# Three blocks in one kernel: two token lists for the experts, list numbers read by GpSimd, and a first phase in a new order

## The chip, the cores and the metric

The kernel runs on one core of a Trainium2 chip. The metric is the device time of one launch, in microseconds (us); the time before is the median of three runs. Engines: TensorE (PE, and PEld for its weight loads), VectorE (DVE), ScalarE (ACT), GpSimd (POOL), and SyncE (SP), which only issues transfers. SPq and POOLq are the queues of SP and GpSimd.

## What is computed

Three independent results, all in float32 at the interface:

```python
# 1. gated linear attention, B=4 H=8 S=768 D=48; a = complex gate, limited to |a| <= 0.999
for t in range(S):
    S_re, S_im = a[t] * (S_re + i S_im) + k[t] outer v[t]
    y[t] = q[t] @ S_re
# 2. a dense block on x of N=3072 rows, DM=384, DFF=2048
y = softplus(x @ w_in) @ w_out
# 3. eight experts, top 1, on N=3072 rows, F2=1024
e_idx = argmax(x @ w_gate + modality_bias[modality_id])
out[mask_e] = gate_w[mask_e] * (relu(x[mask_e] @ w1[e]) @ w2[e])
```

Here the three are chained: the attention's y is the x of the dense block, and its y is the x of the experts.

## The kernel before

All three blocks are matmuls whose operands are split into a high and a low part (`xh`, `xl`, `w`, `gh`, `gl`), three products each. The work has two phases.

**Phase 1** (to about 743 us) runs attention, the dense block, the router and three early pairs of expert tiles interleaved. Each is written as generators (`Attn`, `Moe1`, `Early`) that announce their next operation (`Op`: engine, estimated duration, what it needs, ring places it takes, due unit). `Streams.run` (L148) asks all of them for the time at which they could start, takes the engine that can start first, and among that engine's candidates the one with the smallest `due - LEAD`. A candidate may be chosen although it starts up to `PATIENCE` nanoseconds later than the first. `LEAD` has three numbers a stream, for the first unit, the middle and the last; a stream that has no entry has zeros. The result is a fixed order of instructions for each engine. The clock that `run` advances (`end`, L122) knows an engine's duration, a bus for transfers and at most eight transfers in flight; a transfer counts as landed 900 ns after the bus has moved it.

Tokens go in 24 tiles of 128 (`n`); two tiles make a unit `m` of 256 tokens (12 units) and a group `g` of the attention (12 groups). Of a group:

- `decays` and `products` (L255, L331) make gates and gated q and k on VectorE and ScalarE. The last product, L380, releases 24 loads by SP's queue (`stack`, L390: 12 for each tile, 6 of `ks`, 6 of `qs`), which lay k and q out by head.
- `scores` (L399): TensorE's `pa` (L414) needs the `ks` and `qs` of the tile; VectorE masks the result (`at`, L422).
- `outputs` (L439): `py` on TensorE; ScalarE and VectorE copy it to `y` (L465, L468); two moves on SP's queue (L480, y<-y) turn it; `sink` (L576) splits it into `xh` (L585, ScalarE) and `xl` (L587, VectorE).
- The dense block: `hs` (L613), `softplus` (L626 to L637), `gh` (L644), `gl` (L652), `ys` (L669 to L671).
- The router (`router_unit`, L690): rank of each token within its expert (`pr`, L725 to L729), then its place `di` (L758), and two scatters by GpSimd, one for each tile of the unit, which write the token numbers (`tok`) into a DRAM list `lst` at these places (L762). Both write the same tensor, so that the second waits until the first has landed. `x2d`, L740, stores the tokens' rows.

`Early` takes three pairs of tiles of 256 tokens when ten of the twelve units are routed: a table of offsets, the list entries (`fids`, L1166 to L1168, SP), gathers (`fx`, GpSimd), transposes (`fxt`), weights (`fes`, `few0h/l`, `few1h/l`), first products (`feh`, L1248), relu (`frh` L1259, `frl` L1261), second products (`fey`, L1279), results (`fo`, L1289) and their scatter to `out` (L1292). In names such as `frl13` or `few0l21` the first figure of the last two is the pair and the second the quarter of its hidden columns.

**Between the phases** VectorE makes the table of the remaining pairs (`table`, L796, some 50 small operations up to L872) when the last unit is ranked. `begin` (L1034) loads the first weights (`est`), splits them (`w0h`, `w0l`, `w1h`, `w1l`; L931, L936), reads the lists of the first three pairs (`load_ids`, L893, SP) and gathers their rows (`gather`, L905), and transposes the first pair (`ext`, L954; `exh`, `exl`). **Phase 2** (`Moe2.run`, L1070) is ordered by hand: `eh` (L976), relu, `ey` (L1024), results, scatter to `out` (L1031). A list is read on SP's queue at an offset that SP loads from the table:

```python
o = nc.sync.value_load(self.c["tab"][0:1, 1, s:s + 1], min_val=0, max_val=E * RS)
nc.sync.dma_start(ids[:, :n], self.lst[bass.ds(o, n * P)].rearrange("(p k) o -> p (k o)", k=n))
```

Of the kernel before, what the change touches and what calls it, by code (L numbers as in the profile page):

```python
# [24 lines left out]
P = 128  # L25
# [30 lines left out]
LEAD = dict(load_a=(40.235, 77.705, -53.959), load_qk=(5.175, 62.509, -31.682), decays=(16.662, -1.332, -76.619), products=(1.104, -28.277, -61.848), scores=(-31.933, 17.078, -33.279), outputs=(-39.509, 5.144, 14.553), load_w=(-26.207, 60.684, -77.629), split_w=(46.815, 84.855, 60.651), gate_w=(31.817, -31.456, 89.703), hs=(2.837, 86.252, 46.309), logs=(61.552, 28.125, -11.984), softplus=(53.029, 53.679, -34.061), highs=(-86.34, 1.631, -25.826), lows=(26.821, 19.731, -34.925), ys=(-12.292, -83.704, -79.285), evac=(-55.587, 17.06, 15.15), router=(-2.963, -42.318, 24.777), prepare=(1.018, 90.264, 20.598))  # L56
PATIENCE = (36, 0, 148)
# [4 lines left out]
class Op:  # L62
# [5 lines left out]
    def __init__(self, eng, ns, after=None, take=(), key=None, free=(), lat=None, due=None,  # L68
                 rows=1.0, moves=()):
        self.moves = moves  # L70
# [18 lines left out]
def dma(xfer, k=1, ns=470, **kw):  # L89

    return Op("S", k * ns, moves=[xfer] * k, **kw)

# [8 lines left out]
class Streams:  # L101
# [82 lines left out]
class Attn:  # L184
# [8 lines left out]
    def __init__(self, tc, ctx, a_in, qk_in, v_in, consts, psum):  # L193
# [10 lines left out]
        self.first = self.wp.tile([P, H * 64], F32, tag="v", name="first")  # L204
# [291 lines left out]
class Moe1:  # L496
# [193 lines left out]
    def router_unit(self, m):  # L690
# [80 lines left out]
class Moe2:  # L771
# [133 lines left out]
    def gather(self, s):  # L905
        nc = self.nc
        ids = self.rows[s][0]
# [126 lines left out]
    def begin(self, dynamic=True):  # L1034
# [17 lines left out]
        def tokens():  # L1052
            for s in self.order[:3]:
                yield dma(50, 1, 1500, after=["table", ("lst", NM - 1)], key=("fi", s), due=NM)
                self.load_ids(s)
            for s in self.order[:3]:
                yield Op("G", 1300 * 2, after=[("fi", s), ("x2d", NM - 1)], key=("fx", s), lat=3000)
# [64 lines left out]
class Early:  # L1122
# [11 lines left out]
    def table(self):  # L1134
# [27 lines left out]
    def tokens(self):  # L1162
        nc = self.nc
        for j in range(NE):
            yield dma(50, 1, 1500, after=["early table", ("lst", EU - 1)], key=("ei", j), due=NM + j)
            o = nc.sync.value_load(self.c["early"][0:1, 1, j:j + 1], min_val=0, max_val=E * RS)  # L1166
            self.ids[j] = self.p.tile([P, 2], I32, tag="ids", name=f"fids{j}", bufs=NE)
            nc.sync.dma_start(self.ids[j], self.lst[bass.ds(o, 2 * P)].rearrange("(p k) o -> p (k o)", k=2))  # L1168

    def gathers(self):  # L1170
        for j in range(NE):
            place = Place("ex")
            yield Op("G", 1300 * 2, after=[("ei", j), ("x2d", EU - 1)], take=[place], key=("fg", j), lat=3000, due=NM + j)
# [108 lines left out]
    def evac(self):  # L1282
# [12 lines left out]
    def streams(self):  # L1295
        return (self.table(), self.tokens(), self.gathers(), self.xts(), self.loads(), self.splits(), self.mm1s(), self.relus(),
                self.mm2s(), self.evac())
# [102 lines left out]
def build(ctx, tc, i, out):  # L1400
# [6 lines left out]
    lst = dr.tile([E * RS + 2 * P, 1], I32, name="lst")  # L1407
# [16 lines left out]
    def prepare(room):  # L1424

        n = (E * RS + 2 * P) // P
        pad, mi, rest = room[:, :n].bitcast(I32), room[:, 256:256 + 2 * NT].bitcast(I32), room[:, 320:]
        zero, bb, mf, fl = [rest[:, k * 32:(k + 1) * 32] for k in range(4)]
# [10 lines left out]
        yield dma(120, 4, key="given")  # L1439
# [3 lines left out]
        nc.sync.dma_start(lst.rearrange("(p k) o -> p (k o)", p=P), pad)  # L1443
# [18 lines left out]
    with ExitStack() as s2:  # L1462
        with ExitStack() as s1, ExitStack() as sr, ExitStack() as se, ExitStack() as sa, ExitStack() as sw, tc.manual_schedule():
# [26 lines left out]
            def late():  # L1490
# [4 lines left out]
                for g in ex.begin():  # L1495
# [6 lines left out]
                        prepare(attn.first), early(), late())  # L1502
# [45 lines left out]
def slow(ctx, tc, i, c, dr, x2d, lst, out):  # L1548
# [6 lines left out]
    with ExitStack() as s:  # L1555
# [6 lines left out]
        nc.sync.dma_start(lst.rearrange("(p k) o -> p (k o)", p=P), pad)  # L1562
# [30 lines left out]
def host_inputs(q, k, v, a_re, a_im, moe_w_in, moe_w_out, moe2_modality_id, moe2_w_gate, moe2_modality_bias,  # L1593
# [22 lines left out]
        "tok": tok.T.astype(i32),  # L1616
# [23 lines left out]
```

## Time and profile before

| | us |
|---|---|
| median of three runs | 999.04 |
| the three runs | 994.08, 999.04, 1004.93 |
| the profiled execution | 1004.99 |
| its span | 1003.2 |
| its mean granted clock | 0.973 of full speed |

The profile is of one execution. Busy times are of instructions of an engine; a number in square brackets behind a row is the engine's idle time just before it, and what released it. "x8" says how many instructions a row stands for. In the table of stretches PEclk is the granted TensorE clock, in parts of full speed. Durations of transfers in SPq rows are the time that the queue was occupied with issuing them. The program's names stand without their numbers; the figures of a tile behind a name are left out in the trace.

### The profile page before, as it was taken

Reading aid. Unit: us, or ns where it says so; the run is one execution under the profiler, and the core shown is the slowest. Engines: PE = TensorE matmul, PEld = TensorE weight load, DVE = VectorE, ACT = ScalarE, POOL = GpSimd, SP = SyncE. Lnnn points to the kernel's source line nnn. Section 1 sums busy time; section 2 is a strip of 40 time slices with the busy share of each in tenths; the row PEclk is TensorE's granted clock in tenths of the full one; section 3 lists DMA queues with packets and bytes.
Section 4 is the critical chain, followed back from the end, with each engine's and each line's share of the span. In section 5 each row is a group of like instructions: output and inputs, shape, how many; then the busy total and the mean of one; then the engine's idle time right before and its main releaser. Section 6 shows DMA issues by size and latency. Waiting matters only on the chain. (4 is left out here: it accounts for less than half of the span.)

```text
span 1003.2 us, 17451 instructions
## 1 busy us (share of the span) xinstructions
PE 867.9 (87%) x6377; PEld 827.2 (82%) x6377; DVE 765.9 (76%) x1682; ACT 588.5 (59%) x1041; POOL 91.8 (9%) x94
## 2 busy tenths in 40 slices
PE   1544688999899989999988999999987989999993
PEld 1334688989898889999887899989976989999983
DVE  6999798999799989999877798354467356566582
ACT  4554376575757575766755746465554356555682
POOL 0000000000000000000000000021016022221120
PEclk9999899999999999999989999999998989999997
DMA  9602304141414231332322331251285563542640
GB/s 338 278 1 57 126 25 128 43 126 46 123 40 129 51 118 43 126 101 68 95 74 61 77 91 47 77 151 43 64 289 190 189 245 124 170 150 97 221 163 17
DMA packets 71379, 115.37 MB, mean 115 GB/s; under 512 B 12438, under 2 KB 54989, under 8 KB 68722
## 3 DMA queue, kind: packets, MB, share of 16 engines
q1 hardware_dynamic: 66930, 103.80, 32.2%
q0 software_dynamic: 4352, 10.36, 3.2%
q8 instruction: 52, 0.85, 0.4%
q14 instruction: 45, 0.37, 0.2%
HBM read 93.85 MB, written 10.44 MB: 104 GB/s over the span
## 5 line engine op out<-in xcount | busy, mean ns | idle before, releaser
L613 PE MATMUL h<-xh,w 128*128 128x256 f32 x1152 | 223.2, 287 | 15.7 <-DVE t L637 10.8
L613 PEld LDWEIGHTS h<-xh,w 128*128 128x128 f32 x1152 | 185.0, 192 | 21.2 <-DVE t L637 13.3
L613 PE MATMUL h<-xl,w 128*128 128x256 f32 x576 | 164.1, 285 | 2.9 <-DVE xl L587 2.8
L669 PE MATMUL y<-w,gh 128*128 128x392 f32 x384 | 137.1, 357 | 0.7 <-ACT gh L644 0.7
L671 PE MATMUL y<-w,gl 128*128 128x392 f32 x384 | 131.4, 342 | 1.7 <-DVE gl L652 1.7
L670 PE MATMUL y<-w,gh 128*128 128x392 f32 x384 | 131.4, 342 | 0.0
L613 PEld LDWEIGHTS h<-xl,w 128*128 128x128 f32 x576 | 110.4, 192 | 4.1 <-DVE xl L587 4.1
L626 ACT ACTIVATE t<-h 128x512 f32<-128x512 f32 x96 | 57.1, 595 | 70.9 <-PE h L613 44.7
L762 POOL DMA_INDIRECT lst<-c_tok,di x24 | 25.9, 1078 | 678.0 <-DVE di L758 623.8
L936 DVE TENSOR_TENSOR w1l<-est,w1h 128x768 fp32r<-128x768 f32 x52 | 47.9, 953 | 51.4 <-ACT w1h L931 42.2
L652 DVE TENSOR_TENSOR gl<-t,gh 128x512 fp32r<-128x512 f32 x96 | 65.9, 687 | 20.1 <-ACT gh L644 19.8
L637 DVE SCALAR_TENSOR_TENSOR t<-h,t 128x512 f32<-128x512 f32 x96 | 65.9, 686 | 17.2 <-ACT t L630 15.6
L644 ACT CAST gh<-t 128x512 fp32r<-128x512 f32 x96 | 59.2, 618 | 33.3 <-PE y L670 25.1
L669 PEld LDWEIGHTS y<-w,gh 128*128 128x128 f32 x384 | 72.6, 189 | 3.9 <-issue 2.7
L671 PEld LDWEIGHTS y<-w,gl 128*128 128x128 f32 x384 | 72.3, 188 | 3.0 <-DVE gl L652 2.9
L670 PEld LDWEIGHTS y<-w,gh 128*128 128x128 f32 x384 | 72.6, 189 | 0.0
L976 PE MATMUL eh<-exh,w0h 128*128 128x256 f32 x216 | 61.6, 285 | 4.5 <-DVE erl L980 4.5
L414 PE MATMUL pa<-qs,ks 96*128 96x128 f32 x384 | 53.5, 295 | 13.3 <-DMA qs<-qk 9.5
L414 PEld LDWEIGHTS pa<-qs,ks 96*128 96x128 f32 x384 | 49.1, 206 | 17.3 <-issue 9.8
L628 ACT ACTIVATE t<-t 128x512 f32<-128x512 f32 x96 | 60.7, 633 | 2.0
L630 ACT ACTIVATE t<-t 128x512 f32<-128x512 f32 x96 | 60.8, 633 | 1.8
L976 PE MATMUL eh<-exl,w0h 128*128 128x256 f32 x216 | 61.7, 286 | 0.0
(377 smaller groups left out, 2175.5 us busy)
## 6 DMA issues: line engine op xcount, KB each, us to landing
est<-in_w SPq DMA_DIRECT2D x26, 1536.0 KB
raw<-in_w SPq DMA_DIRECT2D x16, 768.0 KB
a<-in_a SPq DMA_DIRECT2D x12, 768.0 KB
qk<-in_qk SPq DMA_DIRECT2D x12, 768.0 KB
ks<-a SPq DMA_DIRECT2D x144, 64.0 KB
qs<-qk SPq DMA_DIRECT2D x144, 64.0 KB
fes<-in_w SPq DMA_DIRECT2D x24, 384.0 KB
v<-in_v SPq DMA_DIRECT2D x24, 256.0 KB
```

Of the source, the lines that this page charges most:

```text
L414: nc.tensor.matmul(ps[:, h * CH:(h + 1) * CH], K[:, hh * 4 + h], Q[:, hh * 4 + h], start=True, stop=True)
L613: nc.tensor.matmul(ph[:, j], l, r, start=k == 0, stop=k == 3 * KC - 1)
L626: nc.scalar.activation(u, self.h[t][0], AF.Abs)
L628: nc.scalar.activation(u, u, AF.Exp, scale=-1.0)
L630: nc.scalar.activation(u, u, AF.Ln, bias=1.0)
L637: self.nc.vector.scalar_tensor_tensor(u, self.h.pop(t)[0], 0.0, u, ALU.max, ALU.add)
L644: self.nc.scalar.copy(gh, self.t[t][0])
L652: self.nc.vector.tensor_tensor(gl, self.t.pop(t)[0], self.gh[t][0].bitcast(F32), ALU.subtract)
L669: nc.tensor.matmul(py[tt][:, :XW], h, wh, start=f == 0, stop=False)
L670: nc.tensor.matmul(py[tt][:, :XW], h, wl, start=False, stop=False)
L671: nc.tensor.matmul(py[tt][:, :XW], l, wh, start=False, stop=f == FC - 1)
L976: nc.tensor.matmul(ph[:, j], w[:, u, ci, f], x[:, ci], start=k == 0, stop=k == 8)
```

## The change

- There are two DRAM lists. The tokens of a unit's first tile are scattered into `lst[0]`, which begins filled with N, those of its second tile into `lst[1]`, which begins filled with 0, and their numbers in `tok` are less by N. A reader loads the same stretch of both (`list_part`) and adds them on GpSimd (`entries`). The two scatters of a unit write different tensors.
- The lists of the three early pairs and of the first three later pairs are read by GpSimd's queue: the offset by GpSimd's `value_load`, and two loads. The later lists are read by SP's queue as before, with two loads each.
- The planner: each transfer counts as landed 1500 ns later (`MARGIN`); a unit's scatters count as 1300 ns each on GpSimd with a latency of 6000 and occupy the bus for 3000 (they counted as 4800 each on GpSimd, and nothing on the bus); `LEAD` and `PATIENCE` have new numbers, `LEAD` now has entries for the streams of `Early` and of the start of phase 2 too, and `Early`'s `table` and `evac` are called `early_table` and `stores`.
- Phase 1 thereby has a new order on every engine. What TensorE, VectorE and ScalarE do in it is the same, instruction for instruction; phase 2 stands in the same order as before.

```diff
-LEAD = dict(load_a=(40.235, 77.705, -53.959), ...
-PATIENCE = (36, 0, 148)
+LEAD = dict(load_a=(41.378, 45.525, -41.107), ...
+MARGIN = 1500
+PATIENCE = (0, 0, 221)
...
+def list_part(nc, eng, pool, lst, o, n, name, bufs):
+
+    two = pool.tile([P, MTT, 2], I32, tag="ids", name=name, bufs=bufs)
+    for k in range(MTT):
+        eng.dma_start(two[:, k, :n], lst[k][bass.ds(o, n * P)].rearrange("(p k) o -> p (k o)", k=n))
+    return two
+
+
+def entries(nc, two, n):
+    nc.gpsimd.tensor_tensor(two[:, 0, :n], two[:, 0, :n], two[:, 1, :n], ALU.add)
+    return two[:, 0]
...
-            self.done.append(self.bus + 900)
+            self.done.append(self.bus + 900 + MARGIN)
         if op.moves:
             return t
+        if op.stall:
+            self.bus = max(self.bus, t) + op.stall
...
-        yield Op("G", 4800 * MTT, key=("lst", m))
+        yield Op("G", 1300 * MTT, key=("lst", m), lat=6000, stall=1500 * MTT)
         for tt in range(MTT):
             k = m * MTT + tt
             nc.gpsimd.indirect_dma_start(
-                out=self.lst, out_offset=bass.IndirectOffsetOnAxis(ap=di[:, tt:tt + 1].bitcast(U32), axis=0),
+                out=self.lst[tt], out_offset=bass.IndirectOffsetOnAxis(ap=di[:, tt:tt + 1].bitcast(U32), axis=0),
...
-    def load_ids(self, s):
+    def load_ids(self, s, eng=None):
         nc = self.nc
-        n = self.tiles(s)
-        o = nc.sync.value_load(self.c["tab"][0:1, 1, s:s + 1], min_val=0, max_val=E * RS) if s or self.dynamic else 0
-        ids = self.xp.tile([P, 2], I32, tag="ids", name=f"ids{s}", bufs=8)
-        nc.sync.dma_start(ids[:, :n], self.lst[bass.ds(o, n * P)].rearrange("(p k) o -> p (k o)", k=n))
-        self.rows[s] = [ids]
+        eng = eng or nc.sync
+        o = eng.value_load(self.c["tab"][0:1, 1, s:s + 1], min_val=0, max_val=E * RS) if s or self.dynamic else 0
+        self.rows[s] = [list_part(nc, eng, self.xp, self.lst, o, self.tiles(s), f"ids{s}", 8)]
...
     def gather(self, s):
         nc = self.nc
-        ids = self.rows[s][0]
+        ids = entries(nc, self.rows[s][0], self.tiles(s))
+        self.rows[s][0] = ids
...
             for s in self.order[:3]:
-                yield dma(50, 1, 1500, after=["table", ("lst", NM - 1)], key=("fi", s), due=NM)
-                self.load_ids(s)
+                yield Op("G", 2600, after=["table", ("lst", NM - 1)], key=("fi", s), due=NM, lat=2500)
+                self.load_ids(s, self.nc.gpsimd)
...
-            o = nc.sync.value_load(self.c["early"][0:1, 1, j:j + 1], min_val=0, max_val=E * RS)
-            self.ids[j] = self.p.tile([P, 2], I32, tag="ids", name=f"fids{j}", bufs=NE)
-            nc.sync.dma_start(self.ids[j], self.lst[bass.ds(o, 2 * P)].rearrange("(p k) o -> p (k o)", k=2))
+            o = nc.gpsimd.value_load(self.c["early"][0:1, 1, j:j + 1], min_val=0, max_val=E * RS)
+            self.ids[j] = list_part(nc, nc.gpsimd, self.p, self.lst, o, 2, f"fids{j}", NE)
...
-        "tok": tok.T.astype(i32),
+        "tok": (tok.T - N * (np.arange(NT) % MTT)).astype(i32),
```

Three places show how the order moves. First VectorE around group 5 (the last product is a12 <- a12,pt_5; `di2` is the place of unit 2), before:

```order
L378 TENSOR_TENSOR pt_5_3155<-pz_5_3156,pt_5_3155 128x768
L242 TENSOR_TENSOR a20_2502<-s1_63_3421,s2_63_3422 128x6x16
L244 TENSOR_TENSOR a20_2502<-s1_63_3421,s2_63_3422 128x6x16
L380 TENSOR_TENSOR a12_1869<-a12_1869,pt_5_3155 128x1536
L637 SCALAR_TENSOR_TENSOR t32_3446<-h32_3409,t32_3446 128x512
L238 TENSOR_TENSOR s1_64_3451<-a20_2502 128x192
L240 TENSOR_TENSOR s2_64_3452<-a20_2502 128x192
L758 CAST di2_3496<-er2_2997 128x2
```

and now, where the same product (now L397) follows 44 rows behind the last of these:

```order
L439 TENSOR_TENSOR at81_3128<-pa18_3080,c_mask_70 128x512
L285 SCALAR_TENSOR_TENSOR x_6_3085<-x_6_3085,y_6_3086 128x768
L654 SCALAR_TENSOR_TENSOR t28_3098<-h28_2953,t28_3098 128x512
L775 CAST di2_3155<-er2_2969 128x2
L365 TENSOR_TENSOR a12_1880<-a12_1880,e5_2931 128x1536
```

`di2` has moved from 4 rows behind the product that releases the loads of group 5 to 44 ahead of it. In group 8 it has moved less; now `di5` stands directly ahead of the product of that group (it stood 4 rows behind):

```order
L257 TENSOR_TENSOR s2_94_5269<-a30_4357 128x192
L775 CAST di5_5302<-er5_4907 128x2
L397 TENSOR_TENSOR a22_3734<-a22_3734,pt_8_4964 128x1536
L654 SCALAR_TENSOR_TENSOR t55_5291<-h55_5211,t55_5291 128x512
```

Of the other groups, counted in rows: before, `di0`, `di2`, `di3`, `di4`, `di5` and `di6` stand 11, 4, 8, 3, 4 and 8 rows behind the last product of groups 3, 5, 6, 7, 8 and 9. Now only `di6` stands behind one, by 8.

Second, VectorE behind the last operation of the table, before:

```order
L872 CAST c_mask_69<-t_b_8699 1x15
L936 TENSOR_TENSOR w0l0_8738<-est00_8581,w0h0_8737 128x768 x4
L1261 SCALAR_TENSOR_TENSOR frl13_8655<-feh13_8592,frh13_8654 128x512
L1196 TENSOR_TENSOR fxl2_8505<-fxt21_8726,fxh2_8504 128x3x128
L1228 TENSOR_TENSOR few0l20_8731<-fes020_8530,few0h20_8730 128x768
L1228 TENSOR_TENSOR few1l20_8733<-fes120_8531,few1h20_8732 128x768
L936 TENSOR_TENSOR w1l0_9083<-est10_8582,w1h0_9082 128x768 x4
```

and now:

```order
L889 CAST c_mask_70<-t_b_8762 1x15
L1244 TENSOR_TENSOR few0l21_8790<-fes021_8594,few0h21_8789 128x768
L1244 TENSOR_TENSOR few1l21_8792<-fes121_8595,few1h21_8791 128x768
L1277 SCALAR_TENSOR_TENSOR frl20_8718<-feh20_8655,frh20_8717 128x512
L952 TENSOR_TENSOR w0l0_8808<-est00_8644,w0h0_8807 128x768 x4
L1277 SCALAR_TENSOR_TENSOR frl21_8888<-feh21_8816,frh21_8887 128x512
L952 TENSOR_TENSOR w1l0_9099<-est10_8645,w1h0_9098 128x768
```

`frl13`, `fxl2` and the `few0l20` and `few1l20` stand ahead of the table now (`frl13` 55 rows ahead of its end); the second quarter of pair 2 stands directly behind it. Third, GpSimd from the last unit's scatters to the first gathers of phase 2, before:

```order
L762 DMA lst<-c_tok,di_8658 25856x1 x2
L1292 DMA out<-fo_8815,fids_7769 3072x384
L1292 DMA out<-fo_8816,fids_7769 3072x384
L910 DMA ex_8871<-x2d,ids_8792 128x392 x2
L910 DMA ex_8904<-x2d,ids_8803 128x392 x2
```

and now (the five rows from L913 stand three times, for three pairs, ahead of the first add):

```order
L779 DMA lst_62<-c_tok,di_8721 25856x1
L779 DMA lst_63<-c_tok,di_8721 25856x1
L1308 DMA out<-fo_8794,fids_7738 3072x384
L1308 DMA out<-fo_8795,fids_7738 3072x384
L913 TENSOR_LOAD c_mask
L913 ISA x2
L99 REGISTER_ALU
L99 DMA ids_8850<-lst_62 128x2
L99 REGISTER_ALU
L99 DMA ids_8850<-lst_63 128x2
L104 TENSOR_TENSOR ids_8850<-ids_8850 128x2
L926 DMA ex_8946<-x2d,ids_8850 128x392 x2
```

GpSimd now reads three offsets and issues six loads between the writes of `fo` and the first gather, which SP did before.

## Rows read from the trace of the kernel before

**Rows 1.** The page's first part: busy us, share of the span, instructions.

```profile
PE 867.9 (87%) x6377; PEld 827.2 (82%) x6377; DVE 765.9 (76%) x1682; ACT 588.5 (59%) x1041; POOL 91.8 (9%) x94
```

**Rows 2.** Stretches: us, busy PE, PEld, DVE, ACT, POOL; PEclk; DMA share; GB/s.

```profile
400.00:500.00 100.00, 97.53 (x813) 93.75 (x813) 94.90 (x228) 68.82 (x128) 4.01 (x4) 1.00 0.33 93
500.00:550.00 50.00, 42.49 (x296) 40.53 (x293) 38.67 (x104) 29.45 (x55) 1.95 (x2) 0.90 0.26 75
...
750.00:775.00 25.00, 15.74 (x91) 14.57 (x91) 19.14 (x38) 12.23 (x18) 13.57 (x7) 0.80 0.61 216
...
850.00:900.00 50.00, 50.00 (x358) 50.00 (x357) 31.15 (x40) 28.46 (x46) 12.04 (x11) 1.00 0.41 139
```

**Rows 3.** Waits: engine and its line <- releaser: us in all, times, longest.

```profile
POOL ex L910 <- DMA ids<-lst: 73.1, 9, 18.7
POOL lst L762 <- DMA lst<-c_tok,di: 45.8, 12, 7.8
...
ACT xh L585 <- DMA y<-y: 24.6, 14, 4.1
...
PE pa L414 <- DMA qs<-qk: 9.5, 5, 4.4
```

**Rows 4.** Timeline of GpSimd, 533 to 539: start, us, engine, line, operation.

```profile
533.75 0.96 POOL L762 DMA_INDIRECT lst<-c_tok,di  x1 [49.27 <-DVE di L758]
537.40 0.99 POOL L762 DMA_INDIRECT lst<-c_tok,di  x1 [2.69 <-DMA lst<-c_tok,di]
```

**Rows 5.** Timeline of SP's queue: group 9, one load of it, group 10.

```profile
534.56 9.21 SPq L396 DMA_DIRECT2D qs<-qk  x6
...
539.92 3.21 SPq L396 DMA_DIRECT2D qs<-qk  x1
...
584.62 4.08 SPq L396 DMA_DIRECT2D qs<-qk  x6
```

**Rows 6.** Timeline of TensorE: `pa` rows with idle time before them, 200 to 560.

```profile
246.28 1.91 PE L414 MATMUL pa<-qs,ks 96*128 96x128 f32 x15 [0.91 <-DMA ks<-a]
...
346.72 1.16 PE L414 MATMUL pa<-qs,ks 96*128 96x128 f32 x8 [1.43 <-DMA qs<-qk]
...
399.49 0.68 PE L414 MATMUL pa<-qs,ks 96*128 96x128 f32 x4 [1.33 <-issue]
...
441.04 1.13 PE L414 MATMUL pa<-qs,ks 96*128 96x128 f32 x8 [0.50 <-DMA ks<-a]
...
492.37 1.13 PE L414 MATMUL pa<-qs,ks 96*128 96x128 f32 x8 [1.65 <-DMA qs<-qk]
...
545.85 2.08 PE L414 MATMUL pa<-qs,ks 96*128 96x128 f32 x8 [4.39 <-DMA qs<-qk]
```

**Rows 7.** Timeline of VectorE: the last product of group 9.

```profile
528.96 1.75 DVE L380 TENSOR_TENSOR a<-a,pt 128x1536 f32<-128x1536 f32 x1
```

**Rows 8.** Timeline of TensorE: first products of two tiles, 118 to 513.

```profile
122.70 0.58 PE L613 MATMUL h<-xh,w 128*128 128x256 f32 x1 [4.78 <-ACT xh L585]
...
512.45 0.58 PE L613 MATMUL h<-xh,w 128*128 128x256 f32 x1 [3.12 <-DVE t L637]
```

**Rows 9.** Timeline of TensorE from the last ranks to phase 2.

```profile
743.51 0.21 PE L725 MATMUL pr<-ohb,lt 128*128 128x8 bf16 x2
...
757.03 0.69 PE L1279 MATMUL fey<-few1h,frl 128*128 128x384 f32 x1 [9.28 <-DVE frl L1261]
...
782.21 0.28 PE L976 MATMUL eh<-exh,w0h 128*128 128x256 f32 x1
```

**Rows 10.** Timeline of VectorE: behind the last operation of the table.

```profile
752.83 3.54 DVE L936 TENSOR_TENSOR w0l<-est,w0h 128x768 fp32r<-128x768 f32 x4
```

**Rows 11.** Timeline of SP's queue: the first three lists.

```profile
763.36 2.52 SPq L898 DMA_DIRECT2D ids<-lst  x3
```

**Rows 12.** Timeline of GpSimd: the writes of the second early pair.

```profile
760.53 4.72 POOL L1292 DMA_INDIRECT out<-fo,fids  x1 [3.31 <-ACT fo L1289]
767.64 0.98 POOL L1292 DMA_INDIRECT out<-fo,fids  x1 [2.40 <-DMA out<-fo,fids]
```

More of the change, by code (lines that the diff above doesn't have):

```diff
@@ L68, in __init__ @@
     def __init__(self, eng, ns, after=None, take=(), key=None, free=(), lat=None, due=None,
-                 rows=1.0, moves=()):
-        self.moves = moves
+                 rows=1.0, moves=(), stall=0):
+        self.moves, self.stall = moves, stall
         self.eng, self.ns, self.after, self.take, self.key, self.free, self.due = eng, ns, after, take, key, free, due
@@ L203, in __init__ @@
         self.spare = self.ap.tile([P, 2, UJ, KC, NI, NG], F32, tag="a", name="spare")
-        self.first = self.wp.tile([P, H * 64], F32, tag="v", name="first")
+        self.first = [self.wp.tile([P, H * 64], F32, tag="v", name="first"),
+                      self.wp.tile([P, 4, CH], F32, tag="at", name="first2").rearrange("p h t -> p (h t)")]
         self.loaded, self.stk, self.at, self.kn, self.v, self.e = {}, {}, {}, {}, {}, {}
@@ L1132, in __init__, with early_table @@
         self.ids, self.rows, self.raw, self.w, self.x, self.h, self.r, self.y = {}, {}, {}, {}, {}, {}, {}, {}
-    def table(self):
+    def early_table(self):
         v, c = self.nc.vector, self.c
@@ L1164, in tokens @@
         for j in range(NE):
[L1165 to L1168 removed]
+            yield Op("G", 2600, after=["early table", ("lst", EU - 1)], key=("ei", j), due=NM + j, lat=2500)
+            o = nc.gpsimd.value_load(self.c["early"][0:1, 1, j:j + 1], min_val=0, max_val=E * RS)
+            self.ids[j] = list_part(nc, nc.gpsimd, self.p, self.lst, o, 2, f"fids{j}", NE)
     def gathers(self):
@@ L1172, in gathers @@
             place = Place("ex")
-            yield Op("G", 1300 * 2, after=[("ei", j), ("x2d", EU - 1)], take=[place], key=("fg", j), lat=3000, due=NM + j)
+            yield Op("G", 1300 * 2 + 200, after=[("ei", j), ("x2d", EU - 1)], take=[place], key=("fg", j), lat=3000, due=NM + j)
+            self.ids[j] = entries(self.nc, self.ids[j], 2)
             x = self.p.tile([P, 2, XW], F32, tag="x", name=f"fx{j}")
@@ L1295, in streams @@
     def streams(self):
-        return (self.table(), self.tokens(), self.gathers(), self.xts(), self.loads(), self.splits(), self.mm1s(), self.relus(),
-                self.mm2s(), self.evac())
+        return (self.early_table(), self.tokens(), self.gathers(), self.xts(), self.loads(), self.splits(), self.mm1s(), self.relus(),
+                self.mm2s(), self.stores())
 class SlowAttn:
@@ L1406, in build @@
     x2d = dr.tile([N + 1, XW], F32, name="x2d")
-    lst = dr.tile([E * RS + 2 * P, 1], I32, name="lst")
+    lst = [dr.tile([E * RS + 2 * P, 1], I32, name=f"lst{k}") for k in range(MTT)]
     ident = cp.tile([P, P], F32, name="ident")
@@ L1438, in prepare @@
         nc.gpsimd.memset(pad, N)
-        yield dma(120, 4, key="given")
+        nc.gpsimd.memset(none, 0)
+        yield dma(120, 5, key="given")
         nc.sync.dma_start(mi, i["mod"].bitcast(I32))
@@ L1442, in prepare @@
         nc.sync.dma_start(x2d[N:N + 1].rearrange("o (p d) -> (o p) d", d=4), zero[:XW // 4, :4])
-        nc.sync.dma_start(lst.rearrange("(p k) o -> p (k o)", p=P), pad)
+        for x, p in zip(lst, (pad, none)):
+            nc.sync.dma_start(x.rearrange("(p k) o -> p (k o)", p=P), p)
         T = [P, NT, E]
@@ L1501, in build @@
             streams.run(attn.load_a(), attn.load_qk(), attn.decays(), attn.products(), attn.scores(), attn.outputs(), *moe.streams(),
-                        prepare(attn.first), early(), late())
+                        prepare(*attn.first), early(), late())
         ex.weights(s2, 1, "right")
@@ L1561, in slow @@
         nc.gpsimd.memset(pad, N)
-        nc.sync.dma_start(lst.rearrange("(p k) o -> p (k o)", p=P), pad)
+        none = xp.tile([P, (E * RS + 2 * P) // P], I32, name="sl_none")
+        nc.gpsimd.memset(none, 0)
+        for l, p in zip(lst, (pad, none)):
+            nc.sync.dma_start(l.rearrange("(p k) o -> p (k o)", p=P), p)
         def rows():
```

9 lines of the change are left out of this document (5 added, 4 removed).

## The prediction

> **What bounds the kernel now.** I read the page's first part, then the table of stretches, the list of waits, and last the timelines around the longest waits. TensorE is busy 867.9 of 1003.2 us [rows 1]. The stretches [rows 2] show where the rest is lost: in 400–500 it works 97.5 of 100 us and in 850–900 all 50, but 42.5 of 50 in 500–550, at a granted clock of 0.90, and 15.7 of 25 in 750–775, at 0.80. VectorE stands at 94.9 of 100 in 400–500, so it is a near second in the first phase. The change leaves the work of TensorE, VectorE and ScalarE as it is; it can only fill or open gaps.
>
> The waits [rows 3] name the gaps: TensorE at `pa` for the loads of qs (9.5 us in 5 pieces), ScalarE at `xh` for the y moves (24.6 us in 14), GpSimd 12 times, 45.8/12 = 3.8 us each, for the first scatter of a unit before the second may go, and 73.1 us for list reads.
>
> The `pa` waits have a cause that the change touches. At 533.75 and 537.40 GpSimd issues the two scatters of unit 6 [rows 4]. SP is then in the 24 ks/qs loads of group 9: six qs loads take 9.21 us, one of them 3.21, where six take 4.08 in group 10, with no scatter beside them [rows 5]. Two such stalls cost 5.1 us there, and `pa` starts 4.39 us late. TensorE waits so at the start of groups 3, 5, 6, 7, 8 and 9: 0.91 + 1.43 + 1.33 + 0.50 + 1.65 + 4.39 = 10.2 us [rows 6]. These are the groups in which a unit's `di` stands 3 to 11 VectorE rows behind the group's last product; units 1 and 7, which stand 38 and 19 rows ahead of one, go with no such wait in TensorE's timeline.
>
> The Trainium skill, "DMA: Bandwidth & Descriptors", section Specifications, says that transfers under 512 bytes are read, changed and written back. A scatter writes 128 entries of 4 bytes; the stalled loads agree, though no run here shows the mechanism. By that rule two lists save nothing, as the writes are as many as before.
>
> **The change part by part.** The sum is made against the profiled execution, 1004.99 us, which is 5.95 above the median of 999.04.
>
> *The place of the scatters.* In the new order `di` stands ahead of the next group's last product by 39 rows (unit 0), 15 (1), 44 (2), 11 (3), 31 (4), 1 (5) and 12 (7); unit 6 stays 8 behind. A VectorE row of that stage takes 94.90/228 = 0.42 us [rows 2], so 11 rows and the product itself (1.75 us [rows 7]) are about 6.3 us. A pair of scatters now lasts about two issues of 1 us and one landing of 3.8 [rows 3, 4], 5.8 us, as the second no longer waits for the first. Unit 3 is just through, and groups 3, 5, 6 and 7 lose their waits: 0.91 + 1.43 + 1.33 + 0.50 = **−4.2**. Groups 8 and 9 still have scatters in their loads, and I keep their 6.0. With two lists both stalls (2 × 2.6 us) come sooner and together. Bounds for these two groups: −6.0 if stalls that overlap cost one, +2.6 if the shorter stretch of other VectorE work ahead of the first `at` leaves one more stall open. Whole term −10.2 to −1.6.
>
> *The y moves.* In the new order more ScalarE work stands between each tile's copy of y and its `xh` (by rows times their durations about 1.1 us more per tile). Of 24.6 us of `xh` waits [rows 3] most is hidden; what reaches TensorE is seen at 512.45, 3.12 us [rows 8], with part of a low clock behind it (500–550 loses 7.5 us, 4.4 of them at `pa` [rows 2, 6]). I take that one gap, **−3**; bounds 0 (VectorE, at 94.9%, is late anyway) and −6.
>
> *Start-up.* All 16 splits of raw weights now stand ahead of the first scores, about 4.6 us more VectorE work ahead of the first `xl`; a part of it goes into gaps that VectorE had at the very start. TensorE waited 4.78 us for the first `xh` [rows 8] and will wait some more: **+1**, bounds −2 and +2.
>
> *From phase 1 to 2.* Before, the last ranks' product stands at 743.51 (call it T0) and the first `eh` of phase 2 at 782.21, 38.7 us later [rows 9]. In between VectorE makes the table, until 752.83 [rows 10], and TensorE waits 9.28 us at 757.03 for `frl13`, which stands behind the table and four `w0l`. In the new order `frl13` stands ahead of the table, so that wait goes; but `few0l21` now stands behind the table, and the `feh` of that part need it: table to T0 + 9.3, one split of 0.94, so TensorE waits for about 7 us there instead. Behind it `frl20` to `frl23` stand between the `w0l` and `w1l` blocks, some 5 us of small waits, and `ext` stands directly ahead of `eh`, 3 us uncovered. That gives 35 us from T0 to `eh`, 3.7 less; and about 4.5 us of TensorE's work that stood behind T0 stands ahead of it now. Sum **+1**, bounds −1.5 and +3.
>
> *List reads on GpSimd.* Behind the last scatters GpSimd writes two `fo` tiles to `out`, then per pair reads an offset and issues two loads, and only then come the adds and gathers. On SP three such loads took 2.52 us, 0.84 each, offsets included [rows 11]; on GpSimd an indirect transfer takes 0.96 to 0.99 [rows 4, 12], and I take 0.98 for each of the nine steps: 8.8 us. The `fo` writes went from 760.53 to 768.62, the first 4.72 us long [rows 12], T0 + 17 to T0 + 25; with `frl13` ahead of the table they can be through by T0 + 17. Then the adds begin at about T0 + 26 and the first gather lands, by a scatter's 3.8 us, at T0 + 31. The first `ext` wants it at T0 + 31: just hidden, **0**. Bounds: −1 (the last unit's second scatter need not wait its 7.8 us, the longest [rows 3]) and +13 (each of six loads as slow as SP's disturbed one, 3.21 instead of 0.98 [rows 5]).
>
> The Trainium skill, the same page, section "Issuing engine by pattern", gives plain loads to Sync and only indirect ones to GpSimd; with the first-byte times of its Specifications (about 0.6 and 1 us) the six reads would be an estimated 2.4 us dearer. No row here has a plain load on GpSimd.
>
> *Later pairs.* Each has one more load on SP (0.84) and an add; the gathers are issued two pairs ahead, and 850–900 has TensorE busy for 50 of 50 us [rows 2]: **0**, bounds 0 and +2 (a small tail at each of nine waits of GpSimd for ids [rows 3], not hidden for one pair in four).
>
> Sum: −4.2 − 3 + 1 + 1 + 0 + 0 = −5.2, so 999.8 for an execution like the profiled one; in the terms of the median 999.04 − 5.2 = 993.8, **994 us**.
>
> **The rivals.**
> *A, all transfers hidden.* Later transfers were planned for every DMA, not only those that I followed: all of the 10.2 at `pa` goes, of `xh` the full 6, and the transition wins 1.5 with start-up neutral or 2 better. −10.2 − 6 − 1.5 + 2 = −15.7, or about 984. For it: 500–550 alone loses 7.5 us [rows 2], more than I credit there. Against it: units 5 and 6 stay in the loads.
> *B, GpSimd becomes the bound of the transition: slower.* Six list loads on one queue behind the `fo` scatters, each 3.2 us, bring the first gathers 13 us late; TensorE idles, and its clock falls as in 750–775, to a mean of 0.80 over 25 us [rows 2], of which I take 2 us as its price. −5.2 + 13 + 2 = +9.8: 1009. It decides from a load of about 1 us on, as no slack is left; at 2 us each it costs 6 × 1.02 = 6 us. For it: `fo` scatters of 4.72 us on that queue [rows 12]. Against it: scatters and the second of these writes at 1 us each [rows 4, 12].
> *C, the change does what it says and nothing comes of it.* VectorE is the bound where the waits were; what TensorE does not wait for loads it waits for `at` and `xl`: 999. For it: VectorE at 94.9% in 400–500 [rows 2]. Against it: at 545.85 TensorE was released by a load, not by VectorE [rows 6].
>
> **How the numbers follow.** My forecast has 0.36, A 0.32, B 0.22, C 0.10. One per cent, 10 us, is about what a measurement of this kernel can tell from no change (three runs lay between 994.08 and 1004.93). My forecast's own range is 987 to 1002, of which 0.10 lies below 989; A gives 0.29 of its 0.32 to faster; B 0.18 of its 0.22 to slower, and forecast and C 0.02 for unseen cost. Faster 0.39, slower 0.20, same 0.41. The range reaches from 978 (A with 6 more somewhere in the first phase) to 1010 (B); about 2 in 10 stay outside.
>
> **What would show it.** Right: no wait of over 1 us at `pa` for qs in groups 3, 5, 6 and 7, and some left in 8 and 9; the longest `xh` wait gone; one wait of about 7 us at `feh` in the transition in place of the 9.28 at `fey`; about 35 us from the last ranks to the first `eh`; GpSimd's plain loads about 1 us each. Wrong: `ext` waiting for the gathers (B), `pa` waits in the freed groups though no scatter stands there, or a first phase whose TensorE is busy for less than 97 of 100 us in 400–500.

## The result and the profile after

The changed kernel takes 966.97 us, median of four runs (965.83 to 971.85), against 1000.32 for the kernel before in four: a ratio of 0.968, interval 0.9616 to 0.9744. That is 33 us less where 5 were forecast, and below the range, which began at 978.

The profiled execution took 965.83 us, its span 964.2. It is the quickest of the four, where the profile before is of the slowest run; so the two spans differ by 39 us and the medians by 33. The page's first part answers to [rows 1]:

```profile
PE 859.4 (89%) x6377; PEld 823.0 (85%) x6377; DVE 763.9 (79%) x1682; ACT 587.4 (61%) x1041; POOL 110.3 (11%) x123
```

TensorE has the same matmuls and 8.5 us less busy time; the rest of the 39 us is idle time that it lost. The stretches (columns as in [rows 2]; the last from the last unit's ranks to the first `eh`):

```profile
400.00:500.00 100.00, 99.77 (x839) 96.23 (x838) 96.58 (x236) 69.63 (x131) 3.28 (x2) 1.00 0.29 84
500.00:550.00 50.00, 50.00 (x402) 48.93 (x401) 45.67 (x106) 35.08 (x67) 4.42 (x4) 1.00 0.36 85
714.10:748.00 33.90, 23.27 (x137) 20.86 (x135) 23.73 (x76) 14.79 (x23) 15.08 (x19) 0.90 0.72 236
```

TensorE fills the middle of phase 1; in 500–550 it gained 7.5 us and the granted clock is back at 1.00. The list of waits, the lines that answer to [rows 3]:

```profile
POOL ids L104 <- DMA ids<-lst: 75.6, 10, 17.4
...
ACT xh L602 <- DMA y<-y: 1.0, 3, 0.5
...
PE pa L431 <- DMA qs<-qk: 0.2, 1, 0.2
...
PE h L630 <- DVE t L654: 3.8, 8, 0.9
...
DVE at L439 <- PE pa L431: 4.2, 7, 2.3
```

The last two were before:

```profile
PE h L613 <- DVE t L637: 10.8, 10, 3.1
...
DVE at L422 <- PE pa L414: 15.7, 17, 3.4
```

ScalarE's wait for the y moves fell from 24.6 to 1.0 us, TensorE's for qs from 9.5 to 0.2, its wait at `h` for VectorE's `t` from 10.8 to 3.8, and VectorE's at `at` for `pa` from 15.7 to 4.2. The row of the second scatter that waits for the first is gone. GpSimd and SP's queue around group 9, as in [rows 4, 5]:

```profile
504.63 1.48 POOL L779 DMA_INDIRECT lst<-c_tok,di  x1 [45.56 <-DVE di L775]
506.41 1.02 POOL L779 DMA_INDIRECT lst<-c_tok,di  x1 [0.30 <-issue]
```

```profile
502.10 3.79 SPq L413 DMA_DIRECT2D ks<-a  x6
505.93 3.80 SPq L413 DMA_DIRECT2D qs<-qk  x6
509.78 3.80 SPq L413 DMA_DIRECT2D ks<-a  x6
```

Unit 6's scatters still fall into the loads, as the order said. But no load is held up: six take 3.8 us, not 9.21. TensorE's timeline at the places of [rows 8] and [rows 9]:

```profile
127.79 0.58 PE L630 MATMUL h<-xh,w 128*128 128x256 f32 x1 [4.95 <-ACT xh L602]
...
714.10 0.21 PE L742 MATMUL pr<-ohb,lt 128*128 128x8 bf16 x2
...
724.52 0.58 PE L1264 MATMUL feh<-fxh,few0l 128*128 128x256 f32 x1 [6.60 <-DVE few0l L1244]
...
747.97 0.38 PE L992 MATMUL eh<-exh,w0h 128*128 128x256 f32 x1 [0.57 <-ACT exh L972]
```

Three marks split the 39 us of the spans. The first `h` comes 5.1 us later (127.79 for 122.70). From it to the last ranks take 586.3 us instead of 620.8: −34.5. From there to `eh` 33.9 instead of 38.7: −4.8. What is left, phase 2, takes 216.2 instead of 221.0: −4.8; there a wait of 4.49 us at 810.87 for `erl`, which stood behind a late `w1l` on VectorE, is 0.54 at 774.73:

```profile
810.87 0.58 PE L976 MATMUL eh<-exh,w0h 128*128 128x256 f32 x1 [4.49 <-DVE erl L980]
```

```profile
774.73 0.39 PE L992 MATMUL eh<-exh,w0h 128*128 128x256 f32 x1 [0.54 <-DVE erl L996]
```

(before, then after). GpSimd in the transition of the changed kernel, as in [rows 12]:

```profile
729.32 0.99 POOL L1308 DMA_INDIRECT out<-fo,fids  x1 [9.47 <-DVE w0l L952]
730.43 1.17 POOL L99 DMA_DIRECT2D ids<-lst  x2
732.18 1.11 POOL L99 DMA_DIRECT2D ids<-lst  x2 [0.57 <-issue]
733.94 1.11 POOL L99 DMA_DIRECT2D ids<-lst  x2 [0.65 <-issue]
737.08 0.19 POOL L104 TENSOR_TENSOR ids<-ids 128x2 int32<-128x2 int32 x1 [2.02 <-DMA ids<-lst]
737.95 2.39 POOL L926 DMA_INDIRECT ex<-x2d,ids  x1 [0.68 <-POOL ids L104]
```

Two plain loads take 1.1 to 1.2 us there, an add 0.19; the gaps of 0.57 and 0.65 us between the pairs hold the reads of the offsets.

### The profile page after: what moved, and what is told of

The parts are those of the page before. It is cut to its first block, busy times and chain, and to the rows that moved or that the text cites. A ratio compares the mean times of both kernels' runs of the same rounds, so it can differ in the third digit from the quotient of the medians.

```text
span 964.2 us, 17526 instructions
## 1 busy us (share of the span) xinstructions
PE 859.4 (89%) x6377; PEld 823.0 (85%) x6377; DVE 763.9 (79%) x1682; ACT 587.4 (61%) x1041; POOL 110.3 (11%) x123
## 3 DMA queue, kind: packets, MB, share of 16 engines
q1 hardware_dynamic: 67650, 103.90, 34.5%
## 5 line engine op out<-in xcount | busy, mean ns | idle before, releaser
L630 PEld LDWEIGHTS h<-xh,w 128*128 128x128 f32 x1152 | 183.8, 191 | 14.3 <-DVE t L654 5.4
L779 POOL DMA_INDIRECT lst<-c_tok,di x24 | 32.6, 1358 | 619.0 <-DVE di L775 603.5
L992 PE MATMUL eh<-exh,w0l 128*128 128x256 f32 x216 | 61.5, 285 | 0.0
L1040 PE MATMUL ey<-w1h,erh 128*128 128x384 f32 x176 | 60.6, 344 | 0.0
```

The lines of the kernel that those rows point to most:

```text
L630: nc.tensor.matmul(ph[:, j], l, r, start=k == 0, stop=k == 3 * KC - 1)
L992: nc.tensor.matmul(ph[:, j], w[:, u, ci, f], x[:, ci], start=k == 0, stop=k == 8)
L1040: nc.tensor.matmul(self.py[t], l[:, f], w[:, f], start=f == 0 and i == 0, stop=f == E - 1 and i == 2)
```

## The experiments

The planner's choice can be fixed: the sequence of choices of one kernel is written into the other as a string, and `run` follows it. That separates the order from the code. Phase 1 below is the stretch from the first `h` to the last ranks, each from one profile; the same order and work gave 620.8 and 616.3, so some 5 us of a single profile say nothing, and the ratios decide. Each ratio is against runs of the kernel before that were made beside it.

```diff
+            fixed = next(order, None)
+            if fixed:
+                i = [s[6] for s in live].index(CODES.index(fixed))
+                t = [x for x in can if x[2] == i][0][0]
+            else:
                 t, _, i = min((c for c in can if ...
...
-                        prepare(*attn.first), early(), late())
+                        prepare(*attn.first), early(), late(), order=ORDER)
```

### Lists or order

**The lists alone** (the changed kernel with `ORDER` of the kernel before):

> The lists alone: two lists, added by GpSimd, the first six list reads on GpSimd's queue, with the order of phase 1 of the kernel before, instruction by instruction. Theory O (the new order carries the gain, because it leaves every transfer more time): 988 to 1003 us, the waits at pa for qs (7 us and more in all) and at xh for the y moves (over 20 us) stay. Rival L (one list was the cause: the second scatter's wait and the 3 us stalls of SP's queue that come with it): 970 to 985, no load of ks or qs over 1.5 us any more, and the pa waits gone.

Measured: 1000.06, ratio 1.0027 (0.9989 to 1.0066). xh waits 25.7 us, the longest load 3952 ns. In group 9 the two scatters follow each other at 526.39 and 527.65 without a wait, and six loads still take 8.34 us:

```profile
527.21 8.34 SPq L453 DMA_DIRECT2D qs<-qk  x6
```

So neither two lists nor the reads on GpSimd gain anything in the old order, and the second scatter's wait was not what held SP up.

**The order alone** (the kernel before with `ORDER` of the changed one):

> The order alone: one list, read by SP, with the order of phase 1 of the changed kernel, instruction by instruction. Theory O: 967 to 975, of which 1 to 6 us are the transition, where the last unit's second scatter waits for the first and the first list comes later; the pa and xh waits stay away. Rival L: 985 to 1000, and SP's 3 us stalls come back in the loads of groups 8 and 9, where scatters of units 5 and 6 fall.

Measured: 968.79, ratio 0.9718 (0.9687 to 0.9748). The order is all of the gain that can be told. The changed kernel's median is 2 us lower and its ratio 0.004, which the intervals do not tell from nothing. SP's longest load is 2.6 us, and group 9's loads, with unit 6's scatters among them, take their usual time: none over 1 us.

**List reads by SP** in the changed kernel:

```diff
-                self.load_ids(s, self.nc.gpsimd)
+                self.load_ids(s)
...
-            o = nc.gpsimd.value_load(self.c["early"] ...
+            o = nc.sync.value_load(self.c["early"] ...
```

> The changed kernel, but the six list reads of the early and the first three later pairs are issued by SP at the same place of the program. Theory (these reads are hidden either way): 964 to 971. Rival (on SP's queue they wait behind the weights' loads, and the first gather comes late): 972 to 985, with ext waiting for ex at the start of phase 2.

Measured: 965.68, ratio 0.9689 (0.9668 to 0.9709). Which queue reads them makes no difference that can be measured.

### The scatters

**Without the scatters of units 0 to 6**, in the old order:

```diff
-        for tt in range(MTT):
+        for tt in range(MTT if m > 6 else 0):
...
-        nc.gpsimd.memset(pad, N)
+        nc.gpsimd.memset(pad, 0)
```

> The kernel before in its own order, but the scatters of units 0 to 6 are left out and the list begins filled with 0, so that most entries name token 0; nothing else is less. This prices the scatters that fall into the ks and qs loads. If they cause the pa waits: SP's stalls of 3 us vanish, the waits at pa fall from 10 to under 3 us, and the time by 7 to 12 us, to 988 to 993. Rival (the waits at pa hide others that then come forward): the stalls vanish and the time stays within 3 us of 1000.

Measured: 984.68, ratio 0.987 (0.9844 to 0.9895): 13 us, a little more than was expected, against the 10.2 us that TensorE waited at `pa`. The longest load takes 2.0 us instead of 3.5, VectorE waits 4.8 us at `at` for `pa` instead of 15.7, and phase 1 takes 601.3.

**The scatters held back**, with all of the router that follows them in the stream (`ORDER` of before, the entries of the router behind `di` moved behind the group's last `at`):

> The kernel before with its own order, lists and reads, except that the last two steps of the router (the places di and the two scatters) of units 0, 2, 3, 4, 5 and 6, and what follows them in the router, stand behind the last masking of the scores of the group into whose loads they fell: no scatter falls into the loads of ks and qs of groups 3 and 5 to 9. Theory O1 (scatters among these loads cost phase 1 15 us or more, as their omission showed): 980 to 988 us, waits at pa under 3 us. Rival (the omission gained elsewhere, in the GpSimd queue or the writes themselves): 994 to 1002.

Measured: 994.83, ratio 0.997 (0.9944 to 0.9996). The time is the rival's, but not for its reason: the `pa` waits did fall, to 3.7 us in all, and TensorE, which works in order, now waited 5.2 us at `pr` for the router's `ohb`. So the edit was made again with `di` and scatters as a stream of their own:

```diff
-        yield vec(1)
-        di = self.cp.tile(T3, I32, tag="di", name=f"di{m}")
...
+        self.er[m] = er
+
+    def places(self):
+        nc, c = self.nc, self.c
+        for m in range(NM):
+            yield vec(1, after=[("er", m)])
...
```

> The kernel before in its own order, but with di and the scatters as a stream of their own, so that for units 0 and 2 to 6 they alone stand behind the last masking of the scores of the group into whose loads they fell, and the rest of the router keeps its place (when all of it was held back, TensorE waited 5.2 us for it). Theory O1 (the stalls of SP's queue cost what leaving the scatters out gained): 983 to 989 us, no wait at pa over 2 us, no wait at pr. Rival (leaving them out gained something else, for instance fewer writes): 993 to 1000.

Measured: 988.55, ratio 0.9885 (0.9837 to 0.9932), no `pr` wait over 0.4 us, no load over 1.84 us, phase 1 605.0. What leaving the scatters out gained comes from their place: by the ratios 11 of 13 us, though the five runs lie between 984.58 and 994.84.

**The scatters put back into the loads, in the new order** (`ORDER` of after, `di` and scatters of units 0 and 2 to 5 moved):

> The changed kernel, except that di and the scatters of units 0, 2, 3, 4 and 5 stand as many VectorE rows behind the last product of groups 3 and 5 to 8 as in the kernel before (11, 4, 8, 3, 4), so that they fall into the loads again; nothing else moves. Theory O1: 974 to 984 us, pa waits of 5 us or more in all and loads of 2 to 4 us back on SP's queue. Rival (the new order leaves the loads enough time, and two lists shorten the stalls): 966 to 970, loads disturbed but no pa waits.

Measured: 966.52, ratio 0.9673 (0.9626 to 0.9721). The rival holds, and further than it went: the loads are not even disturbed. In group 8 the scatters are issued 1.75 and 3.16 us behind the group's first load, where it is 1.46 and 2.72 us with the lists alone, and the longest of all 288 loads takes 1.73 us:

```profile
456.58 1.10 POOL L819 DMA_INDIRECT lst<-c_tok,di  x1 [43.59 <-DVE a L301]
457.99 1.09 POOL L819 DMA_INDIRECT lst<-c_tok,di  x1 [0.31 <-issue]
```

```profile
454.83 3.79 SPq L453 DMA_DIRECT2D ks<-a  x6
458.66 3.81 SPq L453 DMA_DIRECT2D qs<-qk  x6
```

In the kernel before the same six qs loads take 7.68 us:

```profile
482.55 7.68 SPq L396 DMA_DIRECT2D qs<-qk  x6
```

So a scatter among the loads is not enough. The traces show what else the old order has there: packets of the kind `instruction`, by that name fetches of program code. These are the packets during the first 12 loads of group 8 (kind: packets, MB, share of 16 engines; q0 has GpSimd's transfers, the scatters), first in the kernel before, 478.7 to 490.3:

```profile
q8 instruction: 1, 0.02, 1.6%
q14 instruction: 1, 0.01, 0.9%
q0 software_dynamic: 64, 0.00, 0.4%
```

without the scatters of units 0 to 6, 467.2 to 475.6:

```profile
q8 instruction: 1, 0.02, 0.8%
```

```profile
471.11 4.49 SPq L396 DMA_DIRECT2D qs<-qk  x6
```

and with the scatters put back in the new order, 454.8 to 462.5, where no `instruction` packet falls:

```profile
q1 hardware_dynamic: 1443, 0.66, 34.1%
q0 software_dynamic: 64, 0.00, 0.6%
```

The q8 packet takes 3.06 us in the first and 1.05 in the second. Its place goes with the order. Every trace of the old order has it 4.9 to 5.2 us behind group 8's first load: it takes 2.75 to 3.76 us in the five with the scatters in these loads, and 1.05 to 1.59 in the six without. Seven of the new order have it 11.3 to 12.0 us behind, away from the scatters, and there it takes 0.95 to 1.33. In all 20 traces each of the 229 loads of ks and qs over 0.9 us overlaps an `instruction` packet. Of the 26 over 2.5 us, 25 have a scatter issued in the 6 us ahead of them as well. So SP is held up for 3 us where a fetch and a scatter meet among its loads, and the new order parts the two. No run moved a fetch by itself, and one packet of the last run (at 234.30, 2.5 us behind a scatter) took only 0.91 us: a meeting is not always dear.

### The y moves

**xh later** (`ORDER` of before; in nine tiles `xh`, and `xl` with it, behind 1 to 4 more ScalarE instructions):

> The kernel before, except that xh of nine of the tiles that waited for their y moves (and xl with it) stands 1 to 4 ScalarE instructions later, still ahead of its first product. Theory O2 (ScalarE, which stands still for 25 us at xh, holds up the softplus chain and so TensorE): 986 to 994 us, waits at xh halved, TensorE's waits at h for t under 7 us. Rival (these waits are hidden, VectorE has the time anyway): 997 to 1001.

Measured: 988.85, ratio 0.989 (0.9822 to 0.9957); xh waits 13.7 us, phase 1 605.5, TensorE's waits at `h` for t 5.1 us. The 11 us of waits that went are worth about as much of the time (interval 4 to 18), although TensorE had shown only some of them.

**Both edits**, with the whole router held back, and with the scatters alone:

> Both edits of the two kernels before this one in the order of the kernel before: scatters out of the loads, xh later. If the two are separate terms they add: 970 to 980 us, so that two small edits give most of the change's gain. If one hides the other: 980 to 988.

Measured: 991.42, ratio 0.9895 (0.9841 to 0.9949), above both ranges, with the 5.2 us at `pr` again.

> The kernel before with the scatters alone held back and xh later in nine tiles. If the two are separate terms (13 and 10 us) they add: 972 to 980 us. If both relieve the same chain of ScalarE and VectorE: 981 to 987.

Measured: 985.09, ratio 0.987 (0.984 to 0.9899): 13 us, not the 20 or so of a sum, as was expected if both relieve the same chain. But 15 us of xh waits are left in it, so that this says little of what the two causes are worth, and nothing certain of whether they add.

**xh earlier in the new order** (`ORDER` of after, `xh` up to two ScalarE instructions earlier in 21 tiles):

> The changed kernel, but xh stands up to two ScalarE instructions earlier in 21 of 24 tiles (never ahead of what precedes it in its tile), so that ScalarE comes to it before the y moves have landed. Theory O2 (waits of ScalarE at xh delay the softplus chain and cost TensorE time): xh waits of 15 us or more, and 974 to 985 us. Rival (the new order has slack for them): 965 to 970 with the waits there.

Measured: 972.21, ratio 0.9737 (0.9704 to 0.9769) where the changed kernel has 0.968. xh waits 14.3 us, and the median is 5 us higher; phase 1 takes 598.8 in the profile. The time lies between the two ranges, and the two intervals meet (0.9704 and 0.9744). So the waits seem to cost time in this order too, but some 5 us for 14 us of them.

**No y moves**, in the old order:

```diff
-            for k in range(2):
-                nc.sync.dma_start(y[64 * k + D:64 * k + 64], y3[64 * k:64 * k + D])
```

> The kernel before without the two y moves of each tile (a third of y is left out of x, so that routing differs and phase 2 may take another time; phase 1 up to the last ranks is what counts). This prices xh's waits and the moves as a whole. Theory O2: xh waits gone, the stretch from the first h to the last ranks shorter by 12 to 22 us (it was 616 to 621). Rival (the seven waits left when xh was put later cost nothing): shorter by 8 us or less.

Measured: 980.70, ratio 0.9796 (0.9751 to 0.9841), phase 1 597.8: 18 to 23 us less than the two profiles of that order. The moves' own work is gone here too, and TensorE's waits at `pa` for ks and qs fell with them, from 11.3 to 7.5 us; so this is the most that the waits can be worth, not their price.

> The same without the scatters of units 0 to 6 as well (the list begins filled with 0). If these two carry phase 1's gain: the stretch from the first h to the last ranks is 583 to 592 us, as in the changed kernel (586.3). If something else has a share of its own: 594 to 602 us.

Measured: 975.79, ratio 0.9744 (0.9696 to 0.9792), phase 1 592.1, at the edge of the range for "these two are all", and 6 us from the 586.3 of the changed kernel. With both gone most of phase 1's gain is there; 6 us are left, about what one profile can err.

### The start and the end

> The changed kernel with the start of phase 1 in the order of the kernel before, up to the first product of the dense block, and all the rest in the new order. The first h stood at 122.7 before and at 127.8 after the change. If the start is a term of its own: 961 to 964 us. Rival (what the later stages need from the start, raw weights and a, comes as late as before and the gain is given back): 966 to 972.

Measured: 967.77, ratio 0.9694 (0.9664 to 0.9725): the first `h` at 122.9, phase 1 594.3. The rival holds: the 5 us gained at the start come back as waits at `h` for t, 10.8 us instead of 3.8.

> The reverse: the order of the changed kernel up to the first product of unit 9, behind it that of the kernel before. If the end is a term of its own: 974 to 981 us, 38 us or more from the last ranks to eh. Rival: 966 to 970.

Measured: 976.26, ratio 0.9778 (0.9743 to 0.9812). So the new phase 1, up to unit 9, is worth 22 us alone, and the end 9 or 10 behind it. The old end brings back the waits at `fey` and at `eh` for `erl`; the 2.87 us at `ext` for a gather belong to this mixture, as the kernel before has no such wait there:

```profile
727.94 0.69 PE L1335 MATMUL fey<-few1h,frl 128*128 128x384 f32 x1 [9.29 <-DVE frl L1317]
...
745.78 0.90 PE L1010 MATMUL ext<-ident,ex 128*128 128x128 f32 x3 [2.87 <-DMA ex<-x2d,ids]
...
784.60 0.58 PE L1032 MATMUL eh<-exh,w0h 128*128 128x256 f32 x1 [4.06 <-DVE erl L1036]
```

> Lists and reads of the changed kernel; the order of the kernel before up to the first product of unit 9 (near 605 us), and behind it the order of the changed kernel (the two differ by 5 planned steps at that place). If the end (last units, transition, start of phase 2) is a term of its own, as the stretches say (4.8 us from the last ranks to eh, 3 to 5 us behind it): 986 to 992 us, about 34 us from the last ranks to eh. Rival (the end is quicker only because what comes before it is): 996 to 1001.

Measured: 997.69, ratio 0.9993 (0.9961 to 1.0024), in the rival's range. Its transition takes 33.8 us and what is behind it is 4 us shorter, as in the changed kernel; but the last ranks come later. Between the second `xh` of unit 9 and the last ranks lie 178.3 us, where the changed kernel has 168.9 and the lists with the old order have 164.5. About 4.5 us of that were forecast, as work that the new end puts ahead of the last ranks. The other 9 are mostly idle time: TensorE stands still for 8.9 us in this stretch, 4.5 of them at `pa` for qs, where it is 1.5 in the changed kernel. So the end's 9 us are shown only behind the new phase 1.

### The planner

```diff
-LEAD = dict(load_a=(41.378, ...
+LEAD = dict(load_a=(40.235, ...
 MARGIN = 1500
-PATIENCE = (0, 0, 221)
+PATIENCE = (36, 0, 148)
```

> The changed kernel, planned with its 1500 ns more for each transfer and its new cost of the scatters, but with the LEAD and PATIENCE of the kernel before. If the planner's later transfers alone keep the waits for loads and y moves away: 968 to 980 us, xh waits under 8 us and pa waits under 4. Rival (the new numbers of LEAD were needed, an order for other numbers is a different one): 985 to 1005.

Measured: 988.16, ratio 0.9898 (0.9863 to 0.9933). The time is the rival's. xh waits 7.9 us, `pa` waits for qs 1.7: the later transfers do keep these waits away, but the order has others (9.5 us at `h` for `xl`).

```diff
-MARGIN = 1500
+MARGIN = 0
```

> The changed kernel, planned with the new LEAD and PATIENCE but without the 1500 ns. If the later transfers are what matters: 978 to 995 us, with xh waits of 15 us or more. Rival (the numbers of LEAD carry the gain): 965 to 972.

Measured: 989.86, ratio 0.9926 (0.9895 to 0.9957), xh waits 14.9 us. With the old `LEAD` and `PATIENCE` the gain is 10 us, without `MARGIN` 7, with both 32: the numbers of `LEAD` go with the transfers that the planner assumes.

## Why the prediction was wrong

*The direction and the places were right, the sizes were not.* The two mechanisms that it named for phase 1, loads held up beside scatters and `xh` ahead of its y moves, are the ones that the change removes. Both terms were sized by the waits that TensorE shows at `pa` and behind `xh`, and that is the step that failed; the end of phase 1, put at +1, is the third term mis-sized, at 9 or 10 us the other way.

- *The place of the scatters, −4.2, with 6.0 kept for groups 8 and 9.* The omission is worth 13 us and the hold-back 11, beyond even the term's own bound of −10.2. A late `pa` also makes VectorE late at `at` (15.7 us before, 4.8 without the scatters), and in 500–550 the granted clock was 0.90 before and 1.00 without them; what either adds is not shown. One of the six waits, the 1.33 us of group 7, has no load as its releaser in its row. Groups 8 and 9 lost their waits too, although unit 6's scatters stayed, and with all put back the new order lost nothing. The step "groups 8 and 9 still have scatters in their loads, and I keep their 6.0" took a scatter in the loads for a sufficient cause. It is not: in the traces a code fetch has to meet it there.
- *The y moves, −3, bounds 0 and −6.* "Most is hidden" was the largest error in phase 1. With 11 of the 24.6 us put away the time is 11 us shorter, and without the moves 20, which is the far end. ScalarE works in order; while it stands at `xh`, the softplus steps of other tiles stand behind it. They reach TensorE under other names than the y moves: 10.8 us of waits at `h` for t, 5.1 with `xh` later and 3.8 in the changed kernel. The reason for the bound of 0, VectorE "late anyway", does not hold: the time came back, and VectorE is busy for 96.6 of 100 us in 400–500 now, where it was 94.9.
- *Start-up, +1.* Until the first `h` it was +5.1, outside the bounds (125.9 to 128.0 us in the traces with the new start, 118.5 to 123.6 with the old one). But the old start in the new order does not return it, so it costs nothing.
- *The transition, +1, bounds −1.5 and +3.* The parts were right: a wait of 6.60 us at `feh` in place of 9.28 at `fey`, 33.9 us to `eh` where 35 were given, and 168.9 us from unit 9's second `xh` to the last ranks where the new phase 1 with the old end has 165.4: 3.5 us moved ahead where 4.5 were given. It missed that phase 2 begins better too (the 4.49 us at 810.87), which the trace of before showed and the prediction did not read. The end as a whole is worth 9 us or 10, where +1 was forecast; the marks above account for some 6 of them (−4.8, −4.8 and the 3.5 the other way in phase 1), and the rest is within what two profiles can err.
- *List reads on GpSimd, 0, and later pairs, 0.* Right: on SP they take 965.68. Rival B, each load at 3.2 us, fell: two took 1.1 us. The adds began at 737.08, T0 + 23.0, where T0 + 26 was worked out. The Trainium skill ("DMA: Bandwidth & Descriptors", section "Issuing engine by pattern") would give these loads to Sync; here neither queue is measurably better.
- *Rival A, all transfers hidden, 984,* was nearest: its sentence (planned later for every DMA) is what the order does, but it added the same direct waits, and came to half of the gain.
- *The rule of read, change and write* (the Trainium skill, the same page, section Specifications), by which two lists save nothing: the lists alone did save nothing, 1.0027. That agrees with it, but does not show the mechanism.

The gain as measured: phase 1 is worth 22 us (ratio 0.9778), the end the 9 or 10 that are left to 0.968; the start, the lists and the reads nothing that can be told. The y moves and the scatters, both left out, are worth 25 us (0.9744), enough for phase 1's 22. How the 22 divide between the two is not shown: alone they gave 11 each, together 13 with 15 us of xh waits left.

*What stays open:* why a code fetch takes 3 us beside a scatter and 1 without, and why SP's loads take longer where one overlaps them. And what the order gains in phase 1 beside the two causes, if anything: 6 us of one profile are too few to tell.

## What to carry to other kernels

A wait on an engine that works in order can cost what stands behind it, not only what the bound engine is seen to wait for. To price it, take the transfer away in an experiment, or count the whole standstill of that engine as the far end of the range, not its visible part. Where a transfer stalls in one order and not in another, read every queue in that stretch, the fetches of program code among them. And where a planner orders the work, what it assumes of a transfer's landing must be what the trace shows, and its other numbers belong to that assumption: changing either alone gave a quarter to a third of the gain here.

## What the runs showed of the hardware

A load of 64 KB takes SP's queue 0.6 us, and up to 2.2 us where a code fetch overlaps it and no scatter is near. With a scatter of 128 entries of 4 bytes on GpSimd a few us ahead of the fetch it took up to 3.99 us, with one list or two. In the new order, where the two seldom meet among the loads, some of GpSimd's own scatter instructions took longer (2.2 to 3.7 us for 0.96).

Two moves of 24 KB each within SBUF, issued at once, let `xh` start 2.6 us after ScalarE's copy at the soonest (326.1 and 423.8 in the trace of before, where ScalarE waited for them). In the order before, one tile's pair started 4.6 us late, behind a store of tokens that stood ahead of it in SP's queue and itself waited 3.8 us for the router; there ScalarE's copy had ended at 408.5:

```profile
411.78 1.28 SPq L740 DMA_DIRECT2D x2d<-x  x2
413.12 1.27 SPq L480 DMA_DIRECT2D y<-y  x2
```

ScalarE came to that tile's `xh` at 417.15 and did not wait, so this delay cost nothing that the trace shows.
